# Row maxima one chunk sooner, denominators' scale on VectorE, mixing six slots later, group 12's mixing on VectorE, in a fused attention and feed-forward block

## The chip, the cores and the metric

The kernel runs on one core of a Trainium2 chip. The metric is the device time of one launch in microseconds (us); the median over several runs is compared.

A core has five engines with a queue of instructions each, worked off in order: TensorE (PE, matmuls; its weight loads are shown apart as PEld), VectorE (DVE), ScalarE (ACT), GpSimd (POOL) and SyncE (SP, which here only issues DMAs). An instruction waits on semaphores for what other engines or DMAs have to deliver, and everything behind it in the same queue waits with it.

## The reference, cut to what matters

One transformer block on x of 2048 rows by 512 columns: an adaptive layer norm, attention with 32 heads of 16 in four segments of 512 rows with a running memory, an output projection, a second layer norm and a GELU feed-forward of 1792.

```python
for s in range(4):
    logits = einsum("bhqd,bhkd->bhqk", qs, ks) * scale + mask
    a_dot = einsum("bhqk,bhkd->bhqd", softmax(logits), vs)
    a_mem = (phi(qs) @ M) / (phi(qs) @ z + 1e-6)
    outs.append(g * a_mem + (1 - g) * a_dot)
    M, z = M + phi(ks).T @ vs, z + phi(ks).sum()
x = x + ga * (concat(outs) @ wo)
h = layernorm(x) * (1 + cb) + sb
x = x + gb * (gelu(h @ w1 + b1) @ w2 + b2)
```

## The kernel before, in words

The program has three stages. First come the layer norm, the projections and the memory (to about 190 us); their results q, k and the memory's part go to DRAM. Then attention (to about 490 us), and then the feed-forward.

**Attention** runs over 32 stacks Q of four heads each (8 stacks for each of the 4 segments), in one iteration per stack. An iteration of stack Q computes:

- the *score maxima* for stack Q+2, in parts S0 to S3 (`s_part`): matmuls att<-kst,qst on PE (L606, L643 to L645), whose masked row maxima DVE takes (L613, L617) into a tile nm;
- the *transposed scores* of stack Q, in parts T0 to T5 (`st_part`): matmuls att<-qst,kst on PE (L693), exponentials pt<-att on ACT (L708, L719), and the causal mask on POOL (L696, here called a mask);
- the product with V of the stack before (`pv_part`, L733), copied by ACT (ts<-pv) and stored to DRAM (TD).

The row maxima have a way of their own: POOL splits them into parts (`m_rows`, L661), PE transposes them (`m_put`, L667), ACT copies them (ms<-pv), and a small DMA writes them into three rows of the stack's qst tile (`m_send`, L675: on SP's queue for Q below 10, on ACT's from then on). The transposed scores of that stack read those rows, so that the maxima are subtracted inside the matmul.

Two stacks make a **group** U (16 groups, 4 per segment). What a group needs after its two stacks: `pv_in` loads the denominators dn and the products opk back from DRAM in another layout, with the memory's part amB for U of 4 and more and its factor rm for U of 12 and more; `den` takes the reciprocal on DVE (L775) and scales it (L776); `den_store` stores it (RD); `rb_in` loads it back spread over 16 rows (rbB, L788); `mix` multiplies opk by rbB and adds amB (L793, L795); `o_hi` copies the result on ACT (oh<-opk); `o_lo` takes the remainder (ol, L810). The output projection (`wo_part`, L821) reads oh and ol. `wo_out` adds x, and X2D holds the sum in DRAM. The second layer norm of a segment loads that back (xt, L556), takes its statistics on DVE, normalizes (`ln2_apply`, L568: on POOL for segment 0, on DVE for 1 to 3) and transposes on PE (`ln2_turn`, L574).

**What sets the order.** An iteration is written as a string of parts and of twenty slots c0 to c19:

```python
ORDER = ('S1 c0 T2 T3 T2 c1 S2 c2 S3 T3 S3 c3 c4 c5 T5 S0 c6 c7 T0 c8 c9 '
         'T1 T4 S2 c10 c11 T5 S1 c12 T4 S0 c13 T0 c14 T1 c15 c16 c17 c18 c19')
```

All steps besides S and T are put into slots by the table PRM. Position 20Q + n is slot n of iteration Q (a negative n, or one above 19, lies in another iteration); for a group, 40U + n counts from iteration 2U. So `'mix': 120` is slot c0 of iteration 2U + 6 and `'rbl': 18` puts `rb_in` 18 slots behind `den`. The entries under `quick` (groups 11 and 13) and `end` (14 and 15) replace the common ones. Steps of one slot are issued in the order in which the program lists them, and each lands in the queues of the engines it uses. Steps left over after the last iteration are put by hand (`rest`) into the first part of the feed-forward.

**The feed-forward** of two segments at a time runs over seven quadruples n of blocks (`quad`), each a set of products by a fast multiplication scheme (L1080), copied by ACT (s L1116 among them), completed by DVE (L1089) and stored to DRAM after GELU (GD). Small steps are hung into it by `bg(n, i, ...)`: step i of quadruple n.

Of the kernel before, what the change touches and what calls it, by code (L numbers as in the profile page):

```python
# [27 lines left out]
PRM = {'turn': 2,  # L28
 'pv': [[31, 0, 0, 512], [36, 1, 128, 512], [37, 2, 256, 512], [38, 3, 384, 512]],
 'pvlast': [[25, 0, 0, 512], [30, 1, 128, 512], [31, 3, 384, 512], [35, 2, 256, 512]],  # L30
 'mrows': -21,
 'mput': -13,
 'stacks': -65,
 'den': 92,
 'dnl': 18,
 'rbl': 18,
 'rdl': 4,
 'tsl': 4,
 'msl': 2,
 'msa': 10,  # L40
 'xol': 6,
 'mix': 120,
 'ohi': 130,
 'olo': 132,
 'quick': {'dnl': 11, 'den': 84, 'rbl': 12, 'mix': 107, 'ohi': 117, 'olo': 119},
 'end': {'dnl': 11, 'den': 84, 'rbl': 7, 'mix': 103, 'ohi': 111, 'olo': 116},
 'wo': [[20 * i + o for i in range(8) for o in (2, 5)]] * 2 + [[20 * i + o for i in range(4) for o in (2, 5, 8, 14)]],
 'wox': -25,
 'mixu': 13,
 'olou': 13,  # L50
 'ht': [498, 506, 514, 523],
 'ht1': 644,
 'ln': [{'in': [388, 397, 408, 417], 'stat': [420, 427, 434, 446], 'rstd': 449, 'on': [460, 467, 481, 487]},
        {'in': [528, 537, 548, 568], 'stat': [566, 576, 586, 596], 'rstd': 603, 'on': [624, 626, 628, 630]}],
# [23 lines left out]
 'mmix': 100,  # L78
 'mp': 0,
 'wout': ['vvvv', 'vava', 'vvvv'],  # L80
 'dens': ['p', 'p', 'p', 'v'],
 'm': [0, 1, 0, 1],
 'mq': 14,
 'pvo': ['a', 'a'],
# [17 lines left out]
def block_kernel(ctx: ExitStack, tc: tile.TileContext, x, wq, wk, wv, wo, betaq, betam,  # L102
                 w1, b1c, w2, b2, ccol, wmod, maskbd, mask8, out):
    nc = tc.nc
    v, act, pool, pe, sp = nc.vector, nc.scalar, nc.gpsimd, nc.tensor, nc.sync
# [96 lines left out]
    with ExitStack() as pa:  # L202
# [124 lines left out]
        for ds in ((0,), (1, 2, 3)):  # L327
# [4 lines left out]
            n = slice(ds[0], ds[-1] + 1)  # L332
# [24 lines left out]
        rest = ((2, 3), (4, 5))  # L357
        msteps = {h: [(i, k) for i in rest[h] for k in range(KB)] for h in range(2)}
        mrows = {}
# [153 lines left out]
        for s in range(NSEG):  # L513
            for tok in PRM["A"][s].split():
                n = int(tok[1]) if len(tok) > 1 and tok[1].isdigit() else 0
# [68 lines left out]
    with ExitStack() as pb:  # L584
# [298 lines left out]
        def r_sub(p, n, e=v):  # L883
            x, y = {"t1": ("b12", "b11"), "t2": ("b22", "t1"), "t3": ("b22", "b12"), "t4": ("b21", "t2")}[n]
            for o, i, j in zip(raw(p, n), raw(p, x), raw(p, y)):
                e.tensor_tensor(out=o, in0=i, in1=j, op=ALU.subtract)
# [10 lines left out]
        def r_lo(p, n):  # L897
            for k in range(2):
                v.tensor_tensor(out=R[n][1][k], in0=raw(p, n)[k], in1=R[n][0][k].bitcast(F32),
                                op=ALU.subtract)  # L900
# [52 lines left out]
        for U in range(16):  # L953
            z = U // 4
            p = {**PRM, **(PRM["end"] if U > 13 else PRM["quick"] if U in (11, 13) else {})}
# [57 lines left out]
        for Q in range(-LEAD // 2, NP // 2 + 1):  # L1013
# [4 lines left out]
            for tok in ORDER.split():  # L1018
                n = int(tok[1:])
# [15 lines left out]
    def rest(U, *names):  # L1035
        for n in names:
            for x in [x for x in left if x[0] == n and x[1] == U]:
                left.remove(x)
                x[2]()

    with ExitStack() as pc:
# [53 lines left out]
        def bg(n, i, f, *a):  # L1095
            bgs.setdefault((n + i // 7, i % 7), []).append((f, a))
# [77 lines left out]
        rest(14, "mem_mix")  # L1174
        r_lo(0, "t2")
        rest(15, "mem_mix")
        for n in ("t3", "t4"):
            r_sub(0, n)
        rest(14, "mix")
        for b in range(4):  # L1180
            wo_x(3, b)

# [31 lines left out]
        for n, i, f, *a in ((0, 0, rest, 14, "o_hi", "o_lo"), (0, 1, w_hi, 0, 2), (0, 1, w_hi, 0, 3),  # L1214
                            (0, 3, r_hi, 0, "t3"), (0, 3, wo_late, 2, 3), (0, 3, r_lo, 0, "t3"), (0, 3, w_hi, 1, 0),
                            (0, 4, w_lo, 1, 0), (0, 4, w_lo, 0, 2), (0, 4, w_lo, 0, 3), (0, 4, load_w1, 2),
                            (0, 4, r_hi, 0, "t4"), (0, 4, rest, 15, "mix", "o_hi"), (0, 4, r_lo, 0, "t4"),
                            (0, 4, rest, 15, "o_lo"), (0, 5, g_out, 0, s1, s1, 0, 0), (0, 6, w_hi, 1, 1),
                            (1, 0, ln2_load, 2), (1, 0, w_lo, 1, 1), (1, 0, r_hi, 0, "b22"), (1, 1, wo_late, 3, 4),
                            (1, 1, w_hi, 1, 2), (1, 1, w_hi, 1, 3), (1, 1, r_lo, 0, "b22"), (1, 2, close_wo),  # L1220
                            (1, 3, w_lo, 1, 2), (1, 3, w_lo, 1, 3)):
            bg(n, i, f, *a)
# [6 lines left out]
                ln2_apply(s, b, v)  # L1229

        bg(3, 2, ln2_load3)
        for s, n in ((2, 2), (3, 4)):
            for b in range(4):
                bg(n, 1 + b, ln2_stats, s, b)
            bg(n, 5, ln2_rstd, s)
            for i in range(2):
                bg(n, 8 + i, ln2_applies, s, 2 * i, 2 * i + 2)
            for d in range(KB):
                bg(n, 12 + d, ln2_turn, s, d, (mm, spare)[d % 2])
# [53 lines left out]
        for p in range(2):  # L1293
            n = FH * p + FH - 1
# [56 lines left out]
        for p in range(2):  # L1351
            for j in range(FH):
                quad(FH * p + j, j == 0)
            n = FH * p + FH - 1
# [3 lines left out]
            for m in range(NM):  # L1358
                s, f = 2 * p + m // FB, m % FB
# [68 lines left out]
```

## Time and profile before

| | us |
|---|---|
| median of three runs | 798.66 |
| the runs | 797.84, 798.66, 805.45 |
| the profiled execution | 800.94 |
| its span, first to last instruction | 799.2 |

The span by stage, with the engines' busy time in us:

| stretch | PE | DVE | ACT | POOL | granted PE clock |
|---|---|---|---|---|---|
| 0 to 192 | 189.48 | 130.34 | 102.46 | 88.49 | 1.00 |
| 192 to 490 | 285.41 | 236.65 | 222.11 | 189.24 | 0.98 |
| 490 to 799 | 303.29 | 186.03 | 149.83 | 46.25 | 1.00 |

A busy PE is not a PE at its peak: the ends of its matmuls are modelled, and a lower granted clock makes them longer. A wait is put down to the operation that released it last. In rows of the timeline, idle time of an engine stands in brackets with its releaser behind `<-`; `SPq` and `ACTq` are DMA issues, not busy time.

### The profile page before, as it was taken

The numbers are of one execution on the slowest core, as the hardware profiler recorded it, in microseconds if no ns is written. First come the engines' busy times: TensorE is split into PE (matmuls) and PEld (weight loads), VectorE is DVE, ScalarE is ACT, GpSimd is POOL, SyncE is SP. The second block draws the span as 40 slices with busy tenths as digits, with TensorE's granted clock in tenths as the row PEclk, the third lists the DMA queues.
The fourth block names the chain that finished last, engine by engine and source line by source line (L and its number), as shares of the span: only waits on it lengthen the run. The fifth ranks groups of instructions, "written<-read, shape, count | busy, mean of one in ns | idle before, by whom it ended". The sixth has DMA issues, their size and how long they took to land.

```text
span 799.2 us, 14063 instructions
## 1 busy us (share of the span) xinstructions
PE 778.2 (97%) x4613; PEld 536.1 (67%) x4613; DVE 553.0 (69%) x1333; ACT 474.4 (59%) x910; POOL 324.0 (41%) x550
## 2 busy tenths in 40 slices
PE   9999999999999999998999979999999999999998
PEld 4877777866444445454554536678888888888887
DVE  6686697458888878887876786776669766533423
ACT  4465545465888877776776655767745436653221
POOL 1347366351478566565875562234000404400000
PEclk9999999999999999999999999999999999999999
DMA  9597857496555567677657754576575734445443
GB/s 337 188 321 237 280 179 237 136 320 194 151 173 178 172 193 209 191 205 222 188 162 211 204 153 133 160 264 212 195 259 175 212 119 158 158 146 171 157 136 116
DMA packets 108817, 156.09 MB, mean 195 GB/s; under 512 B 16324, under 2 KB 55620, under 8 KB 108744
## 3 DMA queue, kind: packets, MB, share of 16 engines
q1 hardware_dynamic: 106758, 153.36, 61.4%
q10 hardware_dynamic: 1986, 1.84, 0.7%
q8 instruction: 36, 0.59, 0.3%
q14 instruction: 37, 0.30, 0.1%
HBM read 93.95 MB, written 60.83 MB: 194 GB/s over the span
## 4 chain that ended last, share of the span: by engine, by line
PE 75%; DMA 6%; POOL 6%; DVE 5%; ACT 4%; issue 3%; SPq 0%; ACTq 0%; DVEq 0%; POOLq 0%
PE bx L1080 8%; PE pv L733 6%; PE att L693 6%; PE q L313 5%; PE bx L1345 5%; PE att L606 5%; PE by L1345 5%; PE bv L1345 5%; PE bv L1080 4%; PE k L313 4%; PE mm L821 3%; PE v L464 3%; DMA qst<-ms 3%; PE spare L1345 2%; PE by L1080 2%
## 5 line engine op out<-in xcount | busy, mean ns | idle before, releaser
L613 DVE CUSTOM_DVE_ANT_0 dump<-att,maskb 128x384 bf16<-128x384 f32 (+2 forms) x328 | 172.6, 575 | 49.9 <-PE att L606 22.9
L708 ACT ACTIVATE pt<-att 128x384 f32<-128x384 f32 (+1 forms) x256 | 127.2, 546 | 23.5 <-PE att L693 15.2
L696 POOL TENSOR_SCALAR_AFFINE_SELECT pt<-pt 128x256 f32<-128x256 f32 x256 | 102.0, 413 | 84.3 <-ACT pt L708 67.9
L693 PE MATMUL att<-qst,kst 99*128 99x256 bf16 (+3 forms) x512 | 108.8, 303 | 6.2 <-DMA qst<-ms 3.4
L693 PEld LDWEIGHTS <-kst 99*128 99x128 bf16 x512 | 44.1, 98 | 73.5 <-issue 42.4
L733 PE MATMUL pv<-pt,V 128*32 128x512 f32 (+1 forms) x992 | 82.3, 444 | 4.4 <-POOL pt L696 4.3
L606 PE MATMUL att<-kst,qst 96*128 96x384 bf16 (+2 forms) x328 | 83.7, 337 | 1.3 <-DVE nm L613 0.6
L865 POOL TENSOR_TENSOR wb<-wa 128x256 f32<-128x256 f32 x24 | 23.1, 962 | 149.4 <-DMA wa<-in_w 125.5
L719 ACT ACTIVATE pt<-att 128x256 f32<-128x256 f32 (+1 forms) x128 | 60.6, 494 | 20.8 <-PE att L693 20.2
L733 PEld LDWEIGHTS pv<-pt,V 128*32 128x32 f32 x992 | 26.3, 110 | 42.0 <-issue 28.2
L136 DVE TENSOR_TENSOR gl<-s,gh 128x512 fp32r<-128x512 f32 x34 | 24.1, 707 | 41.7 <-ACT gh L133 41.7
L133 ACT ACTIVATE gh<-s 128x512 fp32r<-128x512 f32 x34 | 21.3, 628 | 46.3 <-PE spare L1345 16.9
L617 DVE TENSOR_REDUCE nm<-att 128x2 f32<-128x256 f32 (+1 forms) x92 | 43.9, 503 | 3.6 <-PE att L645 2.8
L1085 ACT ACTIVATE s<-s,b1t 128x512 f32<-128x512 f32 x42 | 30.3, 721 | 20.4 <-DVE s L1089 20.4
L606 PEld LDWEIGHTS <-qst 96*128 96x128 bf16 x328 | 27.3, 98 | 13.7 <-issue 9.7
L1089 DVE TENSOR_TENSOR s<-bv,s 128x512 f32<-128x512 f32 x28 | 19.2, 688 | 24.5 <-PE bv L1080 18.8
L509 POOL TENSOR_TENSOR q<-qr,q 128x512 bf16<-128x512 f32 x16 | 18.7, 1166 | 26.9 <-ACT q L508 26.7
L127 ACT ACTIVATE ts<-pv 128x512 f32<-128x512 f32 x31 | 18.5, 597 | 17.3 <-PE pv L733 17.3
L500 POOL TENSOR_SCALAR qp<-qp 128x512 f32<-128x512 f32 x12 | 18.7, 1562 | 24.2 <-ACT qp L495 24.2
L136 DVE TENSOR_TENSOR w1ml<-s,w1mh 128x512 fp32r<-128x512 f32 x18 | 13.0, 720 | 21.9 <-ACT w1mh L133 21.9
L613 DVE DVE_READ_ACCUMULATOR2_ANT nm<- 128x1 f32 x328 | 27.2, 83 | 0.0
L133 ACT ACTIVATE w1mh<-s 128x512 fp32r<-128x512 f32 x18 | 11.3, 628 | 26.2 <-PE spare L1345 11.6
(363 smaller groups left out, 2130.6 us busy)
## 6 DMA issues: line engine op xcount, KB each, us to landing
GD<-s SPq DMA_DIRECT2D x56, 256.0 KB
s<-GD SPq DMA_DIRECT2D x52, 256.0 KB
kst<-KD SPq DMA_DIRECT2D x32, 384.0 KB
qst<-QD SPq DMA_DIRECT2D x32, 384.0 KB
TD<-ts SPq DMA_DIRECT2D x32, 256.0 KB
xt<-X2D SPq DMA_DIRECT2D x28, 256.0 KB
wa<-in_w SPq DMA_DIRECT2D x28, 256.0 KB
QD<-q SPq DMA_DIRECT2D x16, 384.0 KB
```

What stands on the lines that cost most here:

```text
L136: lo_eng.tensor_tensor(out=lo, in0=src, in1=hi.bitcast(F32), op=ALU.subtract)
L313: pe.matmul(ps, a[:, k, 128 * g:128 * g + 128], b[k], start=(k == 0 and i == 0), stop=(k == KB - 1 and i == 2))
L606: pe.matmul(ps, q_of(P, h, i), k_of(P, h, 128 * (i + 1)), start=True, stop=True)
L613: v.tensor_tensor_reduce(out=dump[n_dump[0] % 2][:, :n], in0=src, in1=maskb[:, 512 - n:], scale=-1.0, scalar=-4 * NEG, op0=ALU.add, op1=AL ...
L617: v.tensor_reduce(out=dst, in_=src, axis=AX.X, op=ALU.max, negate=True)
L693: pe.matmul(ps, k[:99, e, 128 * j:128 * j + 128], q[:99, e, 128 * j:512], start=True, stop=True)
L696: pool.affine_select(out=t, in_=t, pattern=pattern, compare_op=ALU.is_ge, fill=0.0, base=0, channel_multiplier=-1)
L708: act.activation(pt[:, h, :], ps[:, :n], AF.Exp, scale=0.25)
L719: act.activation(pt, pv_, AF.Exp, scale=0.25)
L733: pe.matmul(ps[32 * c:32 * c + 32, lo:hi], V[4 * s + j][:, VW * hd:VW * hd + 32], pt[:, c % 2, lo - o:hi - o], start=start, stop=stop)
L1080: pe.matmul(ps, a[:, i, k, :], b[k], start=start and k == 0 and c == 0, stop=k == 1 and c == 2, skip_group_check=not start)
L1345: pe.matmul(ps, a[:, c], w[:, lo:hi], start=(f == 0 and i == 0), stop=(last and i == 2))
```

## The change

It alters numbers of the table and three places in the code:

- `m_rows` from slot c19 to c14, directly behind the last S0 of its stack and ahead of the last T1, and `m_put` from c7 to c5, ahead of a T5 and an S0 (`m_send`, two slots behind it, moves along, from c9 to c7);
- the scale of the denominators (`dens`) of groups 0 to 11 from POOL to DVE; `den` one slot sooner, and `rb_in` two slots sooner (c8 of the iteration ahead of the mixing, not c10);
- `mix`, `o_hi` and `o_lo` six slots later (c6, c16 and c18, not c0, c10 and c12) for the groups without `quick` or `end`; group 12's `mix` and `o_lo` on DVE, not POOL;
- the transposes of segment 0's second layer norm two to four slots later (`ht`; the last one stays);
- in the tail, group 14's mixing ahead of the subtractions for t3 and t4;
- in the feed-forward, the load of segment 2's rows, its statistics and what follows one quadruple later.

```diff
- 'mrows': -21,
- 'mput': -13,
+ 'mrows': -26,
+ 'mput': -15,
...
- 'den': 92,
+ 'den': 91,
...
- 'rbl': 18,
+ 'rbl': 17,
...
- 'mix': 120,
- 'ohi': 130,
- 'olo': 132,
+ 'mix': 126,
+ 'ohi': 136,
+ 'olo': 138,
...
- 'mixu': 13,
- 'olou': 13,
- 'ht': [498, 506, 514, 523],
+ 'mixu': 12,
+ 'olou': 12,
+ 'ht': [502, 509, 516, 523],
...
- 'dens': ['p', 'p', 'p', 'v'],
+ 'dens': ['v', 'v', 'v', 'v'],
...
         rest(14, "mem_mix")
         r_lo(0, "t2")
         rest(15, "mem_mix")
+        rest(14, "mix")
         for n in ("t3", "t4"):
             r_sub(0, n)
-        rest(14, "mix")
...
-                            (1, 0, ln2_load, 2), (1, 0, w_lo, 1, 1), (1, 0, r_hi, 0, "b22"), (1, 1, wo_late, 3, 4),
+                            (2, 1, ln2_load, 2), (1, 0, w_lo, 1, 1), (1, 0, r_hi, 0, "b22"), (1, 1, wo_late, 3, 4),
...
-        for s, n in ((2, 2), (3, 4)):
+        for s, n in ((2, 3), (3, 4)):
             for b in range(4):
                 bg(n, 1 + b, ln2_stats, s, b)
```

SP's queue around the load of group 10's denominators, in iteration 25. The first number in a name is the group's (rbB10, dn11), the last one a counter of the program. Before:

```order
L784 DMA RD10_5068<-dn10_4963 128x32
L830 DMA xb1_3_5095<-in_x 128x512
L751 DMA TD11_4977<-ts23_5101 128x512
L756 DMA dn11_5169<-TD11_4977 128x1x32
L758 DMA opk11_5171<-TD11_4977 128x1x512
L765 DMA amB11_5173<-AMD2_3_116 128x512
L788 DMA rbB10_5187<-RD10_5068 128x1x512
```

and in the change:

```order
L784 DMA RD10_5055<-dn10_4965 128x32
L830 DMA xb1_3_5095<-in_x 128x512
L751 DMA TD11_4979<-ts23_5101 128x512
L788 DMA rbB10_5163<-RD10_5055 128x1x512
L756 DMA dn11_5165<-TD11_4979 128x1x32
L758 DMA opk11_5167<-TD11_4979 128x1x512
L765 DMA amB11_5169<-AMD2_3_116 128x512
```

The load rbB10 moved ahead of the three loads of group 11; for group 12 it moves past those of group 13 in the same way, and past nothing for the other groups but one.

POOL's queue around group 10's mixing, at the turn from iteration 25 to 26 (pt52 and pt53 are the scores of the two halves of stack 26, whose second number is the part; nm the row maxima of a stack). Before:

```order
L696 AFFINE_SELECT pt51_0_5212<-pt51_0_5212 128x2x128
L661 TENSOR_TENSOR nm3_2057<-nm3_2057 128x16 x2
L793 TENSOR_TENSOR opk10_4965<-opk10_4965,rbB10_5187 128x512
L795 TENSOR_TENSOR opk10_4965<-opk10_4965,amB10_4967 128x512
L696 AFFINE_SELECT pt52_1_5249<-pt52_1_5249 128x2x128
L696 AFFINE_SELECT pt53_1_5255<-pt53_1_5255 128x2x128
L776 TENSOR_SCALAR dn11_5169<-dn11_5169,omg_71 128x32
L696 AFFINE_SELECT pt52_3_5289<-pt52_3_5289 128x256
```

and in the change:

```order
L661 TENSOR_TENSOR nm3_2057<-nm3_2057 128x16 x2
L696 AFFINE_SELECT pt51_0_5212<-pt51_0_5212 128x2x128
L696 AFFINE_SELECT pt52_1_5247<-pt52_1_5247 128x2x128
L696 AFFINE_SELECT pt53_1_5253<-pt53_1_5253 128x2x128
L696 AFFINE_SELECT pt52_3_5290<-pt52_3_5290 128x256
L793 TENSOR_TENSOR opk10_4967<-opk10_4967,rbB10_5163 128x512
L795 TENSOR_TENSOR opk10_4967<-opk10_4967,amB10_4969 128x512
L696 AFFINE_SELECT pt52_0_5302<-pt52_0_5302 128x2x128
```

Three masks of the iteration now stand ahead of the mixing, the row maxima ahead of the last mask of the iteration before, and the scale of the denominators (L776) is gone from this queue.

DVE's queue in the tail behind attention, around group 14's mixing (hr and s40 are parts of the second layer norm's result, from which the subtractions make t3 and t4; rt2l belongs to t2). Before:

```order
L899 TENSOR_TENSOR rt2l1_6064<-s21_6090,rt2h1_6062 128x512
L886 TENSOR_TENSOR hr1_0_6001<-hr1_2_6013,hr1_0_6001 128x512
L886 TENSOR_TENSOR hr1_1_6007<-hr1_3_6019,hr1_1_6007 128x512
L886 TENSOR_TENSOR hr0_2_5219<-hr0_2_5219,s40_6092 128x512
L886 TENSOR_TENSOR hr0_3_5281<-hr0_3_5281,s21_6090 128x512
L793 TENSOR_TENSOR opk14_5933<-opk14_5933,rbB14_6041 128x512
L795 TENSOR_TENSOR opk14_5933<-opk14_5933,amB14_5935 128x512
L810 TENSOR_TENSOR ol14_6171<-opk14_5933,oh14_6169 128x512
```

and in the change:

```order
L899 TENSOR_TENSOR rt2l1_6064<-s21_6090,rt2h1_6062 128x512
L793 TENSOR_TENSOR opk14_5933<-opk14_5933,rbB14_6041 128x512
L795 TENSOR_TENSOR opk14_5933<-opk14_5933,amB14_5935 128x512
L886 TENSOR_TENSOR hr1_0_6001<-hr1_2_6013,hr1_0_6001 128x512
L886 TENSOR_TENSOR hr1_1_6007<-hr1_3_6019,hr1_1_6007 128x512
L886 TENSOR_TENSOR hr0_2_5230<-hr0_2_5230,s40_6092 128x512
L886 TENSOR_TENSOR hr0_3_5279<-hr0_3_5279,s21_6090 128x512
L810 TENSOR_TENSOR ol14_6171<-opk14_5933,oh14_6169 128x512
```

The two operations of the mixing passed the four subtractions; the low part ol14 did not.

## The prediction

> **What bounds the kernel now.** I read the page's busy times first, then TensorE's own waits, then the timeline around the longest of them on every engine, then the granted clock there.
>
> ```profile
> PE 778.2 (97%) x4613; PEld 536.1 (67%) x4613; DVE 553.0 (69%) x1333; ACT 474.4 (59%) x910; POOL 324.0 (41%) x550
> ```
>
> TensorE (PE) is busy for 97% of the span, so this change, which takes nothing from PE, can only win waits of PE, and time that a busy PE loses to a lower clock. The list of PE's waits (total us, times, longest) shows how little there is:
>
> ```profile
> PE pv L733 <- POOL pt L696: 4.3, 2, 3.0
> PE att L693 <- DMA qst<-ms: 3.4, 3, 1.6
> PE att L693 <- ACT pt L719: 2.1, 2, 1.9
> PE bx L1080 <- ACT s L1116: 1.2, 2, 1.0
> PE bv L821 <- DVE ol L810: 0.9, 1, 0.9
> PE att L574 <- POOL xt L568: 0.6, 1, 0.6
> PE bv L821 <- ACT oh L127: 0.5, 1, 0.5
> ```
>
> Together 13.0 us, in a few places. The ACT wait and the POOL wait have one origin. Group 10 first (columns: start, length, engine, line, tile, in brackets the idle time before and its releaser):
>
> ```profile
> 414.96 0.60 SPq L756 DMA_DIRECT2D dn<-TD  x1
> 416.80 0.59 SPq L788 DMA_DIRECT2D rbB<-RD  x1
> ...
> 424.23 1.27 POOL L793 TENSOR_TENSOR opk<-opk,rbB 128x512 f32<-128x512 f32 x1 [4.87 <-DMA rbB<-RD]
> 425.58 1.26 POOL L795 TENSOR_TENSOR opk<-opk,amB 128x512 f32<-128x512 f32 x1
> ...
> 426.87 0.63 ACT L127 ACTIVATE oh<-opk 128x512 fp32r<-128x512 f32 x1 [1.75 <-POOL opk L795]
> 427.83 0.59 PE L693 MATMUL att<-qst,kst 99*128 99x512 bf16 x2 [1.89 <-ACT pt L719]
> ```
>
> The load of group 10's denominators (rbB) is issued behind three loads of group 11, lands 7.4 us later, POOL stands at the mixing for 4.87 us, ACT at the copy oh behind it for 1.75, and PE at the scores for 1.89, because the exponentials queue behind oh. Group 12 repeats it near the end of attention:
>
> ```profile
> 458.62 0.57 SPq L788 DMA_DIRECT2D rbB<-RD  x1
> 466.68 1.28 POOL L793 TENSOR_TENSOR opk<-opk,rbB 128x512 f32<-128x512 f32 x1 [4.31 <-DMA rbB<-RD]
> 474.97 1.05 PE L733 MATMUL pv<-pt,V 128*32 128x512 f32 x4 [1.28 <-POOL pt L696]
> 479.07 1.92 PE L733 MATMUL pv<-pt,V 128*32 128x512 f32 x4 [3.05 <-POOL pt L696]
> ```
>
> POOL never recovers from its 4.31 us, and PE waits twice for masks (pt L696). Each place has a second price. Stretches of the windows view (length, busy of PE, PEld, DVE, ACT, POOL, then the granted clock):
>
> ```profile
> 428.88:432.29 3.41, 3.41 (x26) 1.49 (x19) 1.04 (x4) 1.55 (x4) 2.81 (x7) 0.50 0.76 173
> 476.66:483.49 6.83, 4.42 (x13) 1.83 (x13) 2.10 (x3) 1.47 (x3) 4.96 (x10) 0.50 0.40 105
> ```
>
> Behind both, PE runs at half clock: 3.41 us and 4.42 busy us at 0.50, so 1.7 and 2.2 us lost. [...]
>
> **The change part by part.**
>
> *Group 10* (load two slots sooner, mixing 6 later). The load now stands ahead of group 11's three, so it is issued by 414.96, nearly two us sooner and with nothing of theirs ahead of it; mixing moves 6 of 20 slots of an 8.9 us iteration, 2.7 us. Together 4.5 us against a stall of 4.87: the rest lands on POOL where nobody waits. Gone: 1.89 + 1.7 = **3.6**. Low end 1.9, without the clock.
>
> *Group 12* (the same, and mixing and its low part on VectorE, DVE). POOL's stall goes, with three of its operations: 1.28 + 3.05 + 2.2 = **6.5**; low end 4.3. DVE takes three operations of about 0.69 (499.62 and its neighbours, below), 2.1 us, some of them longer beside POOL. What hides them:
>
> ```profile
> 483.49 0.69 DVE L839 TENSOR_TENSOR xb<-mm,xb 128x512 f32<-128x512 f32 x1 [4.74 <-PE mm L821]
> ```
>
> DVE had 4.74 us idle there waiting for PE; with PE 4.3 us sooner this is nearly used up. If it is gone, it costs up to the 2.1; the layer norm of segment 1 on DVE would then be late for its transposes.
>
> *Group 14* (mixing ahead of four subtractions in the tail):
>
> ```profile
> 496.43 1.28 DVE L886 TENSOR_TENSOR hr<-hr,hr 128x512 f32<-128x512 f32 x2
> 497.63 1.28 DVE L886 TENSOR_TENSOR hr<-hr,s 128x512 f32<-128x512 f32 x2
> 498.83 0.68 DVE L793 TENSOR_TENSOR opk<-opk,rbB 128x512 f32<-128x512 f32 x1
> 499.62 0.69 DVE L795 TENSOR_TENSOR opk<-opk,amB 128x512 f32<-128x512 f32 x1
> 501.01 1.39 DVE L810 TENSOR_TENSOR ol<-opk,oh 128x512 fp32r<-128x512 f32 x1 [0.70 <-ACT oh L127]
> ```
>
> PE waited 0.5 for oh and 0.9 for ol. Mixing comes 2.4 us sooner, which frees oh; ol still stands behind the subtractions. Those end at about 498.83 + 1.4 = 500.2, and ol, of 0.7 to 1.39, at 500.9 to 501.6. PE's need was at 501.01 + 1.39 - 0.9 = 501.5, and is at 501.0 without the wait for oh; so up to 0.6 stays: **1.1**, between 0 (the load not there at 496.4, with the subtractions queued behind it) and 1.4.
>
> *Loads of segment 2 one quadruple later* past the stores GD. They leave the place ahead of one store that s L1116 waited for (of 1.2 us), and come to stand ahead of the next. **0.6**, between -1.0 (the same wait one quadruple on) and 1.2.
>
> *Row maxima sooner.* PE's transpose of them (L667), ACT's copy and the small load qst<-ms pass a 128-column score pair and a 512-column pair:
>
> ```profile
> 275.55 0.28 PE L693 MATMUL att<-qst,kst 99*128 99x128 bf16 x2
> 276.10 0.22 PE L667 MATMUL pv<-identb,nm 128*128 128x128 bf16 x1
> ...
> 276.71 5.62 DMA qst<-ms
> 364.82 6.68 DMA qst<-ms
> 444.53 7.75 DMA qst<-ms
> ```
>
> That is 0.55 us per iteration. It counts where PE waits for the load, three times, 3.4 in all; the chain of waits has 5.62 to 7.75 us for a load of a few KB there, so it stands behind the big ones, and an earlier issue may only wait longer. Ends 0 and 3 x 0.55 = 1.65; I take **0.8**. [...] On POOL the subtraction for the maxima now waits for DVE's last maximum with one mask queued behind; that mask is needed by slot c11 of the next iteration, some 5 us on, so I count nothing; uncovered it would be half a us per iteration. On ACT the issue of the load stands ahead of another exponential than before, at the same price; for the first ten it is SP's, and moves past nothing that is due.
>
> *Copy oh at slot c16.* Even iterations, with a mixing, take longer (windows from one output copy to the next):
>
> ```profile
> 307.44:316.36 8.92, 8.89 (x74) 4.52 (x73) 7.07 (x27) 6.99 (x16) 6.86 (x13) 1.00 0.63 186
> 316.36:325.09 8.73, 8.73 (x74) 4.53 (x73) 7.46 (x27) 6.58 (x15) 4.29 (x13) 1.00 0.68 214
> ```
>
> 0.19 x 7 = 1.3 if ACT's waits at oh are all of it, 0 if the copy costs the same elsewhere: **0.8**. The scale of the denominators puts 0.24 us on DVE each even iteration, which has 8.92 - 7.07 = 1.85 free, and takes this from POOL:
>
> ```profile
> L776 POOL TENSOR_SCALAR dn<-dn,omg 128x32 f32<-128x32 f32 x12 | 4.4, 364 | 0.1
> 380.90:408.20 27.30, 26.73 (x221) 13.68 (x219) 21.82 (x84) 21.04 (x46) 25.29 (x38) 1.00 0.67 195
> ```
>
> *Layer norm of segment 0 on POOL* (second row: POOL 25.29 of 27.30). There POOL has 2.0 us to spare, mixing starts 2.7 later, two scales (0.73) go: 2.0 late at worst, while the transposes move 4 slots, 1.8 us. The wait of 0.6 stays about as it is, with PE arriving a little sooner: **-0.4**, between +0.6 and -2.
>
> Sum: 3.6 + 6.5 + 1.1 + 0.6 + 0.8 + 0.8 - 0.4 = **13.0 us**. The profiled execution took 800.94 (span 799.2), 2.3 above the median of 798.66; it would come to 787.9, the median to 785.7. I take **786.5**, nearer to the median, since the waits may be somewhat shorter in the faster executions.
>
> **The rivals.** (a) *POOL's backlog moves on.* With mixing at c6, POOL's masks in iterations 22 to 25 come some 2 us later than needed, PE waits 2 us twice and drops its clock twice (1.7): 7.4 back, about 794. For it: 25.29 of 27.30. Against: a mask has most of an iteration to spare. (b) *The clock's dips have another cause* than these waits: 1.7 + 2.2 stay, about 790.4. [...] Against: the first begins 1.1 us after the wait that ends at 427.83, the second 1.7 us after the one that ends at 474.97, and the page's row of slices shows full clock else. (c) *The change doesn't bring group 12's load sooner*: the transfer took 8.1 us with the DMA engines loaded, DVE stands in POOL's place, and the layer norm behind it makes PE wait as before: 6.5 back, about 793. Against: 2.7 us more distance on each side. (d) *Slower: mixing now stands ahead of the row maxima on POOL.* Mixing (2.53), four masks and the subtraction take
>
> ```profile
> L696 POOL TENSOR_SCALAR_AFFINE_SELECT pt<-pt 128x256 f32<-128x256 f32 x256 | 102.0, 413 | 84.3 <-ACT pt L708 67.9 <-ACT pt L719 13.9 <-PE att L606 0.4
> L661 POOL TENSOR_TENSOR nm<-nm 128x16 f32<-128x16 f32 x64 | 13.7, 214 | 15.9 <-DVE nm L613 13.4
> ```
>
> 2.53 + 4 x 0.41 + 2 x 0.21 = 4.6 us, and PE's transpose is 19 slots (8.5 us) behind c6. It decides once rbB lands 3.9 us after c6, that is 8.0 + 3.9 = 12 us after its issue 18 slots before; then PE stops in each of the eleven iterations in which POOL mixes (groups 0 to 10), say 2 us and a dip of 1.7: 41 us, less the 13 that is saved, about 826. The two slow loads took 7.4 and 8.1, so it is unlikely.
>
> **The numbers.** Forecast 0.66, (a) 0.12, (b) 0.06, (c) 0.08, (d) 0.08. One per cent, 8 us, is what a measurement tells from no change: 790.7 to 806.6. Faster: the forecast, half of (b) and a third of (a): 0.73; slower (d) and what I overlook: 0.09; within: 0.18. The forecast's own range, its terms' ends partly together, is 782 to 790; with (b), (c) and (a) to 794, and 780.5 below, where all upper ends (15.7) meet and the clock holds.
>
> **What would show it.** POOL's rows at L793 with no idle before them over 1 us; no granted 0.50 after the start; no wait of PE for masks at the end of attention; PE's wait for oh gone and for ol under 0.5; even iterations at 8.73; the waits for qst<-ms much as now. It would be wrong if PE stands at L667, if DVE's layer norm rows are what L574 waits for at the end of attention, or if half clock stays without a wait ahead of it.

## The result and the profile after

| | before | changed |
|---|---|---|
| median of 12 runs each, same chip (us) | 800.91 | 792.91 |
| lowest to highest | 797.55 to 805.45 | 791.15 to 798.38 |
| ratio, 95% interval | | 0.9909 (0.9884 to 0.9934) |
| the profiled execution, and its span | 800.94, 799.2 | 791.15 (the lowest of the 12), 789.4 |

The change makes the kernel 0.9% faster, about 7 to 8 us of the 13 that were forecast. By the prediction's own yardstick of one per cent that is just within the band of no change (790.7 to 806.6), to which it gave 0.18; the interval of the ratio lies wholly below 1. Two executions among the later runs took 2704 and 3412 us for no reason that was found; the ratios leave them out, and of one kernel below that was the profiled one, so that its waits can't be shown.

The page's busy time, and TensorE's waits (total us, times, longest), after the change:

```profile
PE 772.4 (98%) x4613; PEld 534.9 (68%) x4613; DVE 558.2 (71%) x1348; ACT 474.0 (60%) x910; POOL 318.5 (40%) x535
```

```profile
PE att L693 <- DVE nm L613: 3.4, 7, 1.4
PE bx L1080 <- ACT s L1116: 2.7, 1, 2.7
...
PE att L693 <- DMA qst<-ms: 1.2, 3, 0.8
...
PE bv L821 <- DVE ol L810: 0.6, 1, 0.6
```

The waits for masks (4.3) and for exponentials (2.1) are gone, and two took their place: 3.4 us for row maxima and 2.7 for ACT's s. First what went right, groups 10 and 12 in the timeline:

```profile
412.24 0.60 SPq L788 DMA_DIRECT2D rbB<-RD  x1
413.38 0.58 SPq L756 DMA_DIRECT2D dn<-TD  x1
...
423.52 1.28 POOL L793 TENSOR_TENSOR opk<-opk,rbB 128x512 f32<-128x512 f32 x1
427.44 0.63 ACT L127 ACTIVATE oh<-opk 128x512 fp32r<-128x512 f32 x1
...
450.00 0.60 SPq L788 DMA_DIRECT2D rbB<-RD  x1
459.89 0.68 DVE L793 TENSOR_TENSOR opk<-opk,rbB 128x512 f32<-128x512 f32 x1
```

The load now stands ahead of dn's, and no row of the mixing or of oh has idle time in brackets. The windows view of the change (columns as in that of before) gives two stacks' iterations, with a mixing and without one, and nearly all of attention:

```profile
306.47:315.74 9.27, 8.94 (x74) 4.56 (x73) 7.98 (x28) 7.12 (x15) 5.86 (x12) 1.00 0.65 181
315.74:324.52 8.78, 8.78 (x74) 4.57 (x73) 7.34 (x27) 6.50 (x15) 4.94 (x13) 1.00 0.68 214
192.00:490.00 298.00, 291.40 (x2376) 154.74 (x2374) 251.92 (x823) 226.92 (x487) 183.67 (x371) 1.00 0.65 187
```

No half clock is left, but the iteration with a mixing takes 9.27 us where it had taken 8.92. The timeline there, on three engines:

```profile
312.04 1.27 POOL L795 TENSOR_TENSOR opk<-opk,amB 128x512 f32<-128x512 f32 x1
...
312.07 0.35 DVE L775 RECIPROCAL dn<-dn 128x32 f32<-128x32 f32 x1
312.45 0.89 DVE L776 TENSOR_SCALAR dn<-dn,omg 128x32 f32<-128x32 f32 x1
313.26 0.54 DVE L613 CUSTOM_DVE_ANT_0 dump<-att,maskb 128x384 bf16<-128x384 f32 x1
...
313.87 0.38 PE L693 MATMUL att<-qst,kst 99*128 99x512 bf16 x1 [0.33 <-DVE nm L613]
...
330.05 1.26 POOL L795 TENSOR_TENSOR opk<-opk,amB 128x512 f32<-128x512 f32 x1
...
330.39 0.97 DVE L776 TENSOR_SCALAR dn<-dn,omg 128x32 f32<-128x32 f32 x1
```

The scale takes 0.89 and 0.97 us, not 0.24. It ends 0.03 and 0.05 us behind POOL's addition (312.45 + 0.89 = 313.34 against 313.31; 331.36 against 331.31), with the second S1's maxima queued behind it and TensorE waiting for those. In the profiles of before and of the change, each of the eight scales on VectorE that took over 0.30 us (0.42 to 0.97) ends within 0.05 us behind an instruction of POOL; why it lasts that long is not shown.

The longest of the seven waits for nm, in group 8, is another matter:

```profile
367.91 0.35 DVE L775 RECIPROCAL dn<-dn 128x32 f32<-128x32 f32 x1 [1.75 <-DMA dn<-TD]
368.30 0.24 DVE L776 TENSOR_SCALAR dn<-dn,omg 128x32 f32<-128x32 f32 x1
...
369.06 0.38 PE L693 MATMUL att<-qst,kst 99*128 99x512 bf16 x1 [1.44 <-DVE nm L613]
```

The scale takes its 0.24 us here. But the reciprocal, one slot sooner, comes 1.75 us ahead of its own load dn, and the same maxima stand behind it. Of the 3.4 us, three waits of 0.33 stand behind scales of 0.89 to 0.97 us beside POOL's addition, and 1.44 is this one.

In the tail, the second new wait:

```profile
515.77 1.93 SPq L556 DMA_DIRECT2D xt<-X2D  x4
517.80 8.43 SPq L1086 DMA_DIRECT2D GD<-s  x4
...
524.67 0.60 ACT L1116 ACTIVATE s<-bx 128x512 f32<-128x512 f32 x1 [5.35 <-DMA GD<-s]
...
525.33 0.50 PE L1080 MATMUL bx<-rt2h,w1mh 128*128 128x512 f32 x1 [2.66 <-ACT s L1116]
```

The four loads of segment 2, 256 KB each, stand directly ahead of the store that has to leave before ACT may write s again.

### The profile page after: what moved, and what is told of

The parts are those of the page before. It is cut to its first block, busy times and chain, and to the rows that moved or that the text cites. A ratio compares the mean times of both kernels' runs of the same rounds, so it can differ in the third digit from the quotient of the medians.

```text
span 789.4 us, 14063 instructions
## 1 busy us (share of the span) xinstructions
PE 772.4 (98%) x4613; PEld 534.9 (68%) x4613; DVE 558.2 (71%) x1348; ACT 474.0 (60%) x910; POOL 318.5 (40%) x535
## 4 chain that ended last, share of the span: by engine, by line
PE 75%; DVE 8%; DMA 8%; ACT 4%; POOL 3%; issue 2%; ACTq 0%; SPq 0%; DVEq 0%
PE bx L1080 8%; PE att L693 6%; PE pv L733 6%; PE q L313 5%; PE bx L1345 5%; PE by L1345 5%; PE bv L1345 5%; PE att L606 5%; PE bv L1080 4%; PE k L313 4%; DMA qst<-ms 3%; PE mm L821 3%; PE v L464 3%; PE spare L1345 2%; PE mm L1345 2%
## 5 line engine op out<-in xcount | busy, mean ns | idle before, releaser
L696 POOL TENSOR_SCALAR_AFFINE_SELECT pt<-pt 128x256 f32<-128x256 f32 x256 | 105.5, 424 | 67.1 <-ACT pt L708 47.3
L606 PE MATMUL att<-kst,qst 96*128 96x384 bf16 (+2 forms) x328 | 83.6, 336 | 1.3 <-DVE nm L613 0.7
L865 POOL TENSOR_TENSOR wb<-wa 128x256 f32<-128x256 f32 x24 | 21.2, 883 | 150.8 <-DMA wa<-in_w 77.2
L733 PE MATMUL pv<-pt,V 128*32 128x512 f32 (+1 forms) x992 | 79.8, 439 | 0.0
L719 ACT ACTIVATE pt<-att 128x256 f32<-128x256 f32 (+1 forms) x128 | 62.1, 491 | 19.2 <-PE att L693 17.6
L733 PEld LDWEIGHTS pv<-pt,V 128*32 128x32 f32 x992 | 25.8, 109 | 40.2 <-issue 34.6
L133 ACT ACTIVATE gh<-s 128x512 fp32r<-128x512 f32 x34 | 21.3, 629 | 46.8 <-PE spare L1345 15.7
L606 PEld LDWEIGHTS <-qst 96*128 96x128 bf16 x328 | 27.0, 98 | 12.8 <-issue 8.5
L661 POOL TENSOR_TENSOR nm<-nm 128x16 f32<-128x16 f32 x64 | 13.7, 215 | 39.6 <-DVE nm L613 36.9
```

Of the source, the lines that this page charges most:

```text
L606: pe.matmul(ps, q_of(P, h, i), k_of(P, h, 128 * (i + 1)), start=True, stop=True)
L696: pool.affine_select(out=t, in_=t, pattern=pattern, compare_op=ALU.is_ge, fill=0.0, base=0, channel_multiplier=-1)
L719: act.activation(pt, pv_, AF.Exp, scale=0.25)
L733: pe.matmul(ps[32 * c:32 * c + 32, lo:hi], V[4 * s + j][:, VW * hd:VW * hd + 32], pt[:, c % 2, lo - o:hi - o], start=start, stop=stop)
```

## The experiments

All twelve runs, with before and the change, at a glance. Attention is the time from the first matmul of L606 to the start of the last one of L733 in the profiled execution, the tail from there to the first matmul of L1345. In brackets behind it stands how long the clock was at half speed in that stretch.

| run | ratio to before (95%) | span | attention | tail |
|---|---|---|---|---|
| before | 1 | 799.2 | 309.7 (10.2) | 84.0 |
| changed | 0.9909 (0.9884 to 0.9934) | 789.4 | 299.1 | 85.0 |
| load_only | 0.9886 (0.9838 to 0.9935) | 789.9 | 299.9 | 82.8 |
| mix_only | 0.9905 (0.9881 to 0.9930) | 792.8 | 302.8 (3.4) | 83.6 (3.4) |
| copy_only | 0.9945 (0.9918 to 0.9972) | 795.9 | 305.2 (6.8) | 84.1 (3.4) |
| den_behind | 0.9892 (0.9861 to 0.9923) | 793.9 | 300.9 (3.4) | 88.2 (6.8) |
| scale_pool | 0.9898 (0.9852 to 0.9943) | 791.0 | 296.6 | 88.5 (6.8) |
| rows_back | 0.9926 (0.9901 to 0.9952) | 794.9 | 302.1 | 87.1 (6.8) |
| loads_back | 0.9886 (0.9851 to 0.9920) | 793.4 | 304.8 (6.8) | 83.1 |
| loads_past_store | 0.9865 (0.9833 to 0.9897) | 788.5 | 300.2 | 82.2 |
| load_copy | 0.9865 (0.9835 to 0.9895) | 787.9 | 299.1 | 82.5 |
| load_copy_rows | 0.9824 (0.9797 to 0.9851) | 789.2 | 299.3 | 83.9 |
| scale_loads_fixed | 0.9836 (0.9809 to 0.9864) | | | |
| changed_again | 0.9889 (0.9862 to 0.9915) | 793.4 | 301.2 | 86.2 |

Ratios of neighbouring rows mostly overlap, so what follows rests on places in the traces, and on ratios only where it says so. Below, iterations are numbered by their m_put: number 16 runs from the 16th m_put to the 17th, which is from within the iteration of stack 14 to the same place in the next.

### Which part carries groups 10 and 12

**load_only**, the kernel before with

```diff
- 'rbl': 18,
+ 'rbl': 16,
```

> The kernel before, with only the load of the denominators two slots sooner, so ahead of the next group's three loads; the mixing stays at c0 on POOL. Theory (the place in the DMA queue makes the landing late): the load lands 5 us or less after its issue instead of 7.4 and 8.1, POOL's stalls at L793 of groups 10 and 12 fall from 4.87 and 4.31 to 2 or less, TensorE's waits for pt L719 and pt L696 fall from 6.4 to 1 or less together; span 7 to 10 us below 799.2. Rival (two slots are too few, the DMA engines are full whatever the order): stalls of 3 us or more stay, waits for masks of 2 us or more stay, span 2 to 4 below.

Issue and mixing of groups 10 and 12 in its timeline:

```profile
413.00 0.60 SPq L788 DMA_DIRECT2D rbB<-RD  x1
419.98 1.28 POOL L793 TENSOR_TENSOR opk<-opk,rbB 128x512 f32<-128x512 f32 x1
...
450.88 0.60 SPq L788 DMA_DIRECT2D rbB<-RD  x1
459.93 1.29 POOL L793 TENSOR_TENSOR opk<-opk,rbB 128x512 f32<-128x512 f32 x1
```

Neither mixing has idle time ahead of it, though it stands at c0 on POOL as before; of TensorE's 6.4 us for pt L719 and pt L696, 0.2 are left, and no half clock. The load comes sooner in two ways. Before, it was issued 2.6 and 3.8 us ahead of the moment at which POOL was free for the mixing (424.23 - 4.87 - 416.80, and the same for group 12); here it is 7.0 and 9.1 us. And by the last update of its semaphore in the trace it lands 5.1 and 5.4 us after its issue, against 7.4 and 7.9 before; the 5 us or less that were expected were just missed. This one number is worth as much as the whole change (0.9886 against 0.9909 and 0.9889).

**mix_only**, the kernel before with

```diff
- 'mix': 120,
- 'ohi': 130,
- 'olo': 132,
+ 'mix': 126,
+ 'ohi': 136,
+ 'olo': 138,
...
- 'mixu': 13,
- 'olou': 13,
+ 'mixu': 12,
+ 'olou': 12,
```

> The kernel before, with only the mixing, the copy oh and the low part six slots later and group 12's mixing and low part on VectorE; the load of the denominators stays behind the next group's three loads. Theory (distance is what was missing, and the six slots alone bring most of it): POOL's stall at L793 of group 10 falls from 4.87 to about 2.2 us, TensorE's 1.89 us for pt L719 goes; group 12's stall moves to VectorE with about 1.6 us and costs TensorE 0 to 1.6; the waits for pt L696 (4.3) go; no granted 0.50 behind either; span about 8 to 10 us below the 799.2 of before. Rival (both halves are needed): VectorE's stall at group 12 makes TensorE wait about as long as before, over 3 us, and half clock stays there; span 3.6 below.

Three rows of its timeline:

```profile
408.24 0.45 PE L574 MATMUL att<-ident,xt 128*128 128x128 f32 x1 [2.03 <-POOL xt L568]
...
465.27 0.86 DVE L793 TENSOR_TENSOR opk<-opk,rbB 128x512 f32<-128x512 f32 x1 [3.78 <-DMA rbB<-RD]
...
471.20 0.50 PE L821 MATMUL mm<-woh,oh 128*128 128x512 f32 x1 [1.99 <-DVE xb L839]
```

Distance does help: no wait for pt is left and group 10 has no stall. But group 12's stall has only moved to VectorE (3.78 us, more than the 1.6 expected), where the output projection waits for 1.99 behind it. And POOL, with the mixing late in its queue and the scale still on it, is late for segment 0's layer norm: 2.03, and attention has 3.4 us at half clock. In the change neither is seen: there the load is early, the scale is off POOL, and the transposes stand two to four slots later. The scale isn't what decides: scale_pool below has it on POOL and no such wait.

**copy_only**, the kernel before with only `ohi` 136 and `olo` 138.

> The kernel before, with only the copy oh and the low part six slots later; mixing at c0 on POOL with the late load. Theory (ACT stands at the copy in iterations with a mixing): iterations 16, 18 and 20 take 8.73 to 8.77 us from one m_put to the next instead of 8.92; ACT's wait for opk in group 10 goes and with it TensorE's 1.89 us and the half clock behind; group 12 stays as it is; span about 4.5 below 799.2. Rival (the copy costs the same elsewhere): iterations 16 to 20 stay at 8.92; only group 10's part goes, span 3.6 below or less.

An iteration with a mixing in its windows view, and a row of its timeline:

```profile
307.55:316.28 8.73, 8.73 (x74) 4.53 (x73) 7.07 (x27) 7.13 (x15) 6.28 (x13) 1.00 0.74 188
```

```profile
439.39 0.82 PE L693 MATMUL att<-qst,kst 99*128 99x384 bf16 x2 [3.89 <-DMA qst<-ms]
```

As the theory has it, iterations with a mixing take 8.73, and TensorE's wait in group 10 is gone although POOL still stands there for 2.96 us. The span fell by only 3.3: in this execution the rows' load was 3.89 us late, with 6.8 us at half clock, and 2.8 us of group 12's waits for masks stay.

### Why the change's iterations got longer

**scale_pool**, the changed kernel with

```diff
- 'dens': ['v', 'v', 'v', 'v'],
+ 'dens': ['p', 'p', 'p', 'v'],
```

> The changed kernel with the scale of the denominators of groups 0 to 11 on POOL again; the reciprocal stays in its new slot ahead of the maxima. Theory (both operations count, 0.35 and 0.26 us): the waits of 0.33 for nm L613 fall to about 0.07, the 1.44 of group 8 to about 1.2 (there the reciprocal itself waited for its data), iterations 16, 18 and 20 take 9.0, span -1.0 to -1.8. Rival (the slot does it and the engine of the scale counts nothing): waits and span as in the changed kernel, 789.4 within 0.5.

The same iteration in its windows view, and two of TensorE's waits:

```profile
306.70:315.48 8.78, 8.78 (x74) 4.57 (x73) 7.04 (x27) 7.01 (x16) 6.22 (x13) 1.00 0.65 196
```

```profile
PE att L693 <- DVE nm L613: 1.5, 3, 0.6
PE pv L667 <- POOL nm L661: 1.1, 2, 0.7
```

9.27 became 8.78: all of the 0.5, more than the theory allowed, since the scale had taken not 0.26 but 0.89 and 0.97 us beside POOL's addition. Group 8's wait fell from 1.44 to 0.61, where 1.2 was expected; the reciprocal still waits for its load there, 1.25 us. Attention, at 296.6, is the shortest of all. On the other side TensorE now stands at L667 for the row maxima of stacks 25 and 26, while POOL normalizes segment 0 as well: a backlog on POOL as in rival (d), at 0.4 and 0.7 instead of 2 us and only there.

**den_behind**, the changed kernel with `den` 92, `rbl` 16, `rdl` 3: reciprocal and scale behind the maxima.

> The changed kernel with the denominators' reciprocal and scale one slot later again (behind the two maxima of the second S1 on VectorE, not ahead of them); their store and their load back stay in the slots of the change. Theory (the reciprocal and the scale hold up these maxima, and TensorE waits for them at the scores): the seven waits of L693 for nm L613, 3.4 us in all, fall below 0.8, iterations 16 to 24 with a group's steps take 9.0 or less from one m_put to the next instead of 9.26 to 9.54, and the span falls by 2.5 to 3.5 us to about 786.5. Rival (the copy oh at slot c16 makes them long): they stay at 9.26 and the span within 0.5 us of 789.4. Second rival (the load of the denominators is late, whatever stands behind it): the 1.44 us of group 8 stay, only the 0.33 ones go, span -1.5.

TensorE's waits:

```profile
PE att L693 <- DMA qst<-ms: 5.0, 6, 2.7
PE bx L1080 <- ACT s L1116: 3.3, 2, 3.1
...
PE att L693 <- DVE nm L613: 0.3, 1, 0.3
```

The waits for nm went as the theory says, group 8's too. The time was not won: the rows' load was late by 5.0 us here, and iterations 16 and 18 took 9.64 and 9.25 with its waits in them, only 20 took 8.77. Whether that is chance or follows from the later scale is open.

### The tail

**loads_back** and **loads_past_store**, the changed kernel with segment 2's loads back in quadruple 1 (and its statistics in 2), or one step further on:

```diff
- (2, 1, ln2_load, 2), (1, 0, w_lo, 1, 1),
+ (1, 0, ln2_load, 2), (1, 0, w_lo, 1, 1),
...
- for s, n in ((2, 3), (3, 4)):
+ for s, n in ((2, 2), (3, 4)):
```

```diff
- (2, 1, ln2_load, 2), (1, 0, w_lo, 1, 1),
+ (2, 2, ln2_load, 2), (1, 0, w_lo, 1, 1),
```

> The changed kernel with the four loads of segment 2's rows and its statistics one quadruple sooner again, as before the change. Theory (the loads now stand on the DMA queue ahead of the store that frees s for L1116): the wait of 2.66 us of bx L1080 for s L1116 goes back to about 0.9, with 0.3 at the quadruple ahead; span -1.4, about 788. Rival (the store is late whatever stands ahead of it, since the first half's output stores were moved nearer as well): the wait stays over 2 us and the span at 789.4.

> The changed kernel with the four loads of segment 2's rows one step later, directly behind the store that L1116 waits for and not ahead of it; statistics as in the change. Theory: no wait of bx L1080 for s L1116 over 0.3 us is left, span -2.4 to -2.8, about 786.8; the layer norm has its rows some 2 us later, which nobody notices. Rival (a place further on waits for the stores that now stand behind the loads): the wait of 2.66 goes and one of 1 to 2 us comes in the same or the next quadruple, span -0.7 to -1.7.

The wait for s L1116 was 1.0 us in the one and 0.9 in the other, each a quadruple earlier (in quadruple 2); at the place of the 2.66 nothing is left. In all five profiles of kernels that have the loads as in the change it was there: 2.7, 3.1, 3.3, 2.4 and 3.1. So the loads' place, directly ahead of the store, makes it; the 0.9 comes from another store, and "no wait over 0.3" was missed. changed_again has that wait in quadruple 2 as well, at 1.0, with no load of segment 2 ahead of it: before, too, the loads need not have caused it. The long span of loads_back has other reasons: 6.8 us at half clock in attention, and this in the tail (POOL's row ahead of VectorE's and TensorE's):

```profile
494.48 1.83 POOL L800 TENSOR_TENSOR amB<-amB,rm 128x512 f32<-128x512 f32 x1 [8.62 <-DMA rm<-rdd]
...
495.08 2.37 DVE L886 TENSOR_TENSOR hr<-hr,s 128x512 f32<-128x512 f32 x2
...
498.11 0.50 PE L821 MATMUL bv<-woh,ol 128*128 128x512 f32 x1 [2.19 <-DVE ol L810]
```

Two of the subtractions ahead of ol take 2.37 us, 1.28 elsewhere, while POOL multiplies. In the seven kernels with group 14's mixing moved, the wait for ol is 0.5 and 0.6 us where L800 begins behind the subtractions (scale_pool, the change), and 1.3 to 2.2 in the five where it begins sooner.

### The row maxima, and a better version

**rows_back**, the changed kernel with `mrows` -21 and `mput` -13.

> The changed kernel with the row maxima back in their old places (m_rows at c19, m_put at c7). Theory (an earlier send brings the rows sooner, us for us): TensorE's waits for qst<-ms rise from 1.2 to about 3 us, span +1.5 to +2.5. Rival (the load waits behind the large ones whenever it is sent): waits for qst<-ms between 0.6 and 1.8, span within 1 of 789.4; the waits for nm L613 (3.4) stay by both.

The waits for qst<-ms were 2.5, between the two bands; those for nm were 6.0, not 3.4. Over all profiles the kernels with the old places wait 2.5 to 4.0 us for that load (six kernels), those with the new ones 0.3, 0.6, 1.2, 1.5, 2.3, 4.1 and 5.0. The 0.3 (loads_back) and copy_only's 3.9 are too low: waits of 1.67 and 1.03 us that the list puts down to VectorE end within 0.05 us behind a landing of these rows. That the earlier send makes the difference of the means isn't shown, since the low values are of kernels in which TensorE waits for nm as well, and so comes later to the rows. The send is 0.7 us sooner, but the loads then take longer: from issue to the last update of the semaphore 4.07 us in the change against 3.72 before, on the mean of the 22 that ACT issues. For stack 21 it is 7.54 against 6.68: more than what was won.

**load_copy** and **load_copy_rows**: the kernel before with `rbl` 16, `ohi` 136 and `olo` 138; then with `mrows` -26 and `mput` -15 as well. **scale_loads_fixed**: the changed kernel with segment 2's loads as in loads_back and

```diff
- (pool if PRM["dens"][U // 4] == "p" else v).tensor_scalar(
+ (pool if U < 10 else v).tensor_scalar(
```

**changed_again** is the changed kernel beside them.

> The kernel before, with the load of the denominators two slots sooner and the copy oh and the low part six slots later, nothing else (three numbers of the table). Theory (these two carry what the change gains in attention): no wait for pt L696 or pt L719 over 0.3 us, iterations 16, 18 and 20 at 8.72 to 8.77 us as with the copy alone, span 1 to 1.5 below the 789.9 of the load alone, ratio to before about 0.987. Rival (the two win the same time): even iterations at 8.9 and a ratio of 0.989 or more.

> As the run with load and copy, and the row maxima in their new places. Theory (rows that are sent 0.66 us sooner land sooner): waits for qst<-ms of 1.2 us or less against the 3.5 to 3.9 that the kernels with the old places have, odd iterations 0.03 longer (8.76 against 8.73, 0.5 us over attention), span about 1.5 below that run, ratio 0.985. Rival (the rows wait behind large loads whenever sent): waits of 2 to 4 us as without, ratio the same or 0.001 higher.

> The changed kernel with the scale of the denominators on POOL for groups 0 to 9 (group 10 and 11 stay on VectorE, where POOL was late for nm L661) and segment 2's loads and statistics where they were before. Theory: iterations 16, 18 and 20 at 8.77, no wait of L667 for nm L661 over 0.3, the wait for s L1116 1 us or less; span 786 to 788, ratio 0.985 to 0.987, clearly below the changed kernel's on the same chip. Rival (the waits are passed on to the rows' load): qst<-ms grows by what goes elsewhere, ratio as the changed kernel's.

> The changed kernel once more, beside the three others. By the ratio known it takes 0.991 of before; waits for nm L613 near 3.4 us and for s L1116 near 2.7 us come back if they belong to the kernel; if they were of that one execution they differ. Half clock: none if the waits stay under 1.5 us, but 1.7 us of loss where one of 2.7 falls so that the clock drops.

TensorE's waits, load_copy_rows first, then changed_again:

```profile
PE att L693 <- DMA qst<-ms: 4.1, 3, 2.5
PE bv L821 <- ACT oh L127: 2.0, 1, 2.0
```

```profile
PE att L693 <- DVE nm L613: 4.6, 9, 1.0
PE bx L1080 <- ACT s L1116: 4.1, 2, 3.1
```

Both new waits of the changed kernel came back: they are its own. Load and copy together do what was expected of them: iterations 16, 18 and 20 take 8.73, ratio 0.9865, though that ratio's interval overlaps with load_only's. With the rows the median is 787.39 us, against 792.58 for changed_again on the same chip, and 0.9824 lies clear of 0.9889: five numbers of the table beat both kernels. The ratio is better than expected, but the way there wasn't shown: its profile has 4.1 us of waits for qst<-ms, not 1.2 or less, and its profiled execution, of 790.91 us, is the longest of its six. scale_loads_fixed, 0.9836, is 4 us below changed_again, with intervals that just touch, which fits what the two new waits cost; its own waits aren't shown.

## Why the prediction was right, and where it failed

The forecast of a gain came true, and its main mechanism with it. The size did not: 792.91 us lies above the forecast's own range (782 to 790). It lies in the wider one, to 794, which was kept for rivals (a) to (c); none of these came, and other terms went wrong instead, so that the number falls there by luck.

**Groups 10 and 12 (3.6 and 6.5):** right, waits and half clock both gone. But the cause is the place of one load in SP's queue; the six slots of the mixing, which the prediction added to it ("together 4.5 us against a stall of 4.87"), and VectorE's part in group 12 were not needed for it. Half clock is priced for an execution in which both dips come; waits as long stand without one as well (below).

**Scale on VectorE, "which has 8.92 - 7.07 = 1.85 free":** the step that failed, together with the reciprocal's earlier slot, for which the sum has no term. Free time over an iteration says nothing of the moment: both now stand ahead of maxima that TensorE needs at once, the scale takes up to 0.97 us beside POOL's addition, and the reciprocal waits for its load. And 0.24 was the median of four cases: beside two of them POOL did nothing, and in a third its mask was through 0.1 us after the scale began. The group's row of before had a warning:

```profile
L776 DVE TENSOR_SCALAR dn<-dn,omg x4: 241/241/872, 448.5 to 495.1; 128x32 f32<-128x32 f32 x4
```

Minimum, median, maximum: the 872 is the fourth, at 485.94, beside POOL's L800 until 486.78. The mixing at c6 brings POOL's addition beside the scale at c11. The mixing there is harmless with the scale on POOL (scale_pool); the scale at c11 with the mixing in its old place was not run. Instead of a gain of 0.8 from the copy (copy_only has 0.18 to 0.20 on each of iterations 14, 16, 20 and 24) there are 3.4 us of waits for nm, 3.1 more than before, and 4.6 in changed_again.

**Loads of segment 2 (0.6, low end -1.0):** the prediction named the mechanism ("the same wait one quadruple on") and chose the wrong side; 1.2 us of waits became 2.7, so -1.4, and in three of five profiles 3.4 or 6.8 us at half clock besides.

**Group 14 (1.1):** the wait for oh went, 0.6 for ol stayed: 0.8 here. Where POOL's L800 falls on the subtractions, 1.3 to 2.2 us for ol stand against 1.5 for oh and ol before, so the move wins 0.2 at best and loses 0.7 at worst. **Row maxima (0.8):** 2.2 between these two profiles, less 0.03 to 0.05 on each iteration; load_copy and load_copy_rows, which differ in them alone, have 4.0 and 4.1. Waits of 4.1 and 5.0 with the early send speak against counting on a gain from it. **Layer norm of segment 0 (-0.4):** the wait of 0.6 is gone. The later transposes are the likely cover; the scale off POOL is not, as scale_pool shows, and the early load was not tried apart from them with the mixing at c6.

By the waits: 10.1 (both groups) + 0.8 - 1.4 + 2.2 - 3.1 + 0.6 = 9.2 of the 9.8 by which the two spans differ; the rest was not traced. The medians differ by 8.0.

One bound of the prediction doesn't follow from its terms: with all upper ends (15.7) the median would come to 783, not to 780.5.

**The signs named:** no idle over 1 us at L793, no half clock, no wait for masks came true in the profile; even iterations at 8.73 did not, the wait for ol was 0.6 and not under 0.5, and the waits for qst<-ms fell from 3.4 to 1.2 where "much as now" was forecast.

**The rivals:** (a) did not come, POOL's masks stay ahead. (b) falls: with these waits gone, no half clock is left in the change and in load_only (granted clock 1.000 in both). (The row of slices that the prediction set against it could not have told: 3.41 us at half clock leave a slice of 20 us at 0.91.) (c) did not come with the load moved; without it (mix_only) it does in part, at 1.99 us. (d) came only as 0.4 and 0.7 us with the scale on POOL, and as 0.2 twice in den_behind.

## What to carry to other kernels

When a stall comes from a late transfer, first look at what stands ahead of it in its DMA queue; here two slots for one load won as much as the whole change. Before moving a short operation to an engine with free time, look at what is queued right behind it, and at what the other engines run in that moment; read the spread of its durations, not only the median. Ask also whether its own input is there by then: a reciprocal one slot sooner stood 1.75 us with everything behind it. Test each part alone, and in pairs: the mixing in its new place costs nothing with the scale on POOL, and 0.5 us an iteration with the scale on VectorE.

## What the runs showed of the hardware

**Half clock, and the waits beside it.** Stretches at half clock in the windows view, of den_behind and rows_back, then 10 us of changed_again at full clock around its wait of 3.1 us:

```profile
372.32:375.73 3.41, 3.41 (x17) 2.17 (x14) 1.20 (x5) 1.54 (x4) 0.41 (x1) 0.50 0.73 228
525.92:532.74 6.82, 5.83 (x14) 4.57 (x15) 4.00 (x9) 4.54 (x8) 0.67 (x1) 0.50 0.64 202
```

```profile
529.96:533.37 3.41, 3.41 (x10) 2.63 (x9) 3.00 (x7) 2.72 (x6) 0.00 (x0) 0.50 0.84 258
```

```profile
526.00:536.00 10.00, 6.86 (x30) 5.55 (x30) 6.12 (x13) 6.04 (x11) 1.54 (x2) 1.00 0.64 202
```

The stretches of before last 3.41 and 6.83 us. The first, from 428.88, begins 1.1 us behind a wait of TensorE of 1.89 us; the second, from 476.66, begins within the wait of 3.05 that ends at 479.07. The length of a wait alone didn't tell whether one comes: waits of 1.90 in load_only, 2.52 in load_copy_rows, 2.66 in the change and 3.1 in changed_again came without half clock (mean granted clock 1.000 in all four), while den_behind, with single waits of 2.7 and 3.1, has 0.994. What decides is not shown.

**VectorE beside POOL.** The scale of 0.24 us takes up to 0.97 beside an addition on POOL in the change. Two subtractions on VectorE take 2.37 instead of 1.28 beside a multiplication there in loads_back. The reciprocal stays at 0.33 to 0.35 in before and in the change, though POOL works beside 13 of the 16 in each.
